# Two blocks' first layer in seven products, a written-out TensorE order, and weights released in three steps

## The chip, the cores and the metric

The kernel runs on one core of one Trainium2 chip. The metric is the device time of one execution in microseconds (us); 312.05 us is the median of five runs of the kernel before, which lie between 306.78 and 312.97 us. The profile shows one of these executions.

## What is computed

For 8 batches and 8 heads, 576 positions of 64 values each, a retention layer without softmax, then a layer with the activation h·cos(h) between two matrix products:

```python
scores = scale * np.matmul(q, k.transpose(0, 1, 3, 2))
ret = scores * Dmat[None]                 # gamma_h ** (i - j), 0 above the diagonal
x = np.matmul(ret, v)                     # then (B*S, H*D) = (4608, 512)
h = x @ w_in                              # 512 -> 2048
out = (h * np.cos(h)) @ w_out             # 2048 -> 512
```

Inputs and output are float32; the kernel multiplies in bf16 and accumulates in float32.

## The kernel before

The 4608 tokens are cut into nine blocks (0 to 8) of 512. For a block, the retention part runs as "sessions" on TensorE, chunks of 64 positions with a running state: `session` (L634 scores, L643 state update, L652 the state's share, L661 the share inside a chunk). Its operands come as float32 tiles through `stgk`, `stgv`, `stgq` (three, three and two buffers), are weighted and cast mostly on POOL (GpSimd) into `natk`, `natv`, `qnat`, and are transposed for the scores by TensorE (L575, L593) or by a DMA (L604). The result is the block's `xt`.

The first layer is `mlp1`: for each of 16 columns f of 128, four matmuls into a PSUM bank (L763, 512 or 256 columns wide; blocks 0 to 2 take it in halves of 256), then ScalarE's sine of the shifted bank (L771, which is the cosine) and VectorE's product into `gt` (L774). So the bank is read twice and free after two operations.

The second layer is `plain2` for block 0 (L800). For blocks 1 to 8 it is `wino2`: a two-by-two block product with seven block products in place of eight (P1 to P7; each 16 matmuls of 256 columns, L886). It needs sums of the left operand (four per half on VectorE, L847 and L853), sums of `w_out` made once (`wsums`, L826), and reuses three PSUM banks: ScalarE takes a copy (`sn`) of a partial sum before TensorE goes on accumulating in the bank, and VectorE adds copy and bank (L898). `store` (L785) issues the output from SP.

The order of the work is made when the kernel is built. `Graph.run` is a list scheduler: every operation has a duration and a wanted time (`prio`), an engine takes what can start first, TensorE's choice also weighs a model of its instruction fetch (`fetched`: 256 instructions at a time, taken to land 6000 ns after they are asked for, three of them 3500 ns later). The engines then run their lists in order, with semaphore waits between them. Buffers come from pools (`POOLS`); those of most pools are handed out in the order of creation. In the first 20 us `warm` (L418) fills TensorE's gaps with matmuls of ones, 128 columns each.

At the start the loads of q, k, v go through SP's queue; `w_in` (four slabs, order 0, 2, 1, 3) and `w_out` (four slabs) are issued by POOL. Slab 0 of `w_in` waits for the first half of the first v tile; the other seven all wait for the second half of the q tile of x = 1 (`graph`, L954 to L958). Here x = 0 and x = 1 are the two pairs of batches that a block takes together. The next tiles of k, q, v (rows 2 and 3) wait for slabs 1 and 3 of `w_out` (`GATE`).

## Time and profile before

| | |
|---|---|
| median of 5 runs | 312.05 us (306.78 to 312.97) |
| the profiled execution | 312.97 us; its span 311.2 us, so 1.8 us lie around the span |
| mean granted TensorE clock | 0.988 of full |
| TensorE matmuls | 295.2 us busy (95%), 4274 recorded |
| VectorE, ScalarE, POOL busy | 206.3, 188.3, 109.8 us |
| first matmul of the first layer | 20.45 us from the span's start |
| end of TensorE's last matmul | 308.0 us |

A row of the groups reads: line, engine, operation, tile written <- tiles read, shape, count | busy us, mean ns of one | idle time just before it and what ended most of it. Matmuls overlap, so a mean of 273 ns is a latency; the rate at which they follow each other is read from the chain of waits, whose rows give start, length and what ran.

### The profile page before, as it was taken

What the parts mean: (1) busy time and instruction counts of PE and PEld (TensorE: products, weight loads), DVE (VectorE), ACT (ScalarE), POOL (GpSimd) and SP (SyncE); (2) the same over time, 40 slices, a digit from 0 to 9 for tenths busy, and PEclk for the clock granted to TensorE, in tenths of its full rate; (3) what the DMA queues carried; (4) which work ended last, traced back from release to release, by engine and by line L of the source; (5) the groups of instructions that cost most, each with busy time, mean ns of one, the idle gap of its engine ahead of it and who ended that gap; (6) DMA issues with size and microseconds to landing.
All of it is one profiled execution on the core that took longest, in us unless ns stands there. A gap on an engine that the chain in (4) does not pass through costs nothing.

```text
span 311.2 us, 10091 instructions
## 1 busy us (share of the span) xinstructions
PE 295.2 (95%) x4274; PEld 215.2 (69%) x4277; DVE 206.3 (66%) x371; ACT 188.3 (61%) x340; POOL 109.8 (35%) x134
## 2 busy tenths in 40 slices
PE   8987999799999999999997799999999999999995
PEld 8876765688777888567854475768646666667684
DVE  3475972475975669898476577775679667665641
ACT  3376743888959786855463566474686765455430
POOL 2261057769627581930470731312742000000000
PEclk9999999999999999999999599999999999999999
DMA  8999999999989899875999539259802100300123
GB/s 168 213 171 206 204 227 192 245 266 222 199 207 207 122 209 263 170 156 143 249 204 264 127 32 243 67 107 200 173 1 72 69 2 0 121 16 2 61 77 136
DMA packets 126397, 46.80 MB, mean 150 GB/s; under 512 B 105104, under 2 KB 122000, under 8 KB 126352
## 3 DMA queue, kind: packets, MB, share of 16 engines
q1 hardware_dynamic: 122128, 41.95, 61.4%
q0 software_dynamic: 4224, 4.19, 8.3%
q8 instruction: 34, 0.56, 0.8%
q14 instruction: 11, 0.09, 0.1%
HBM read 36.70 MB, written 9.44 MB: 148 GB/s over the span
## 4 chain that ended last, share of the span: by engine, by line
PE 88%; ACT 3%; issue 2%; DVE 2%; DMA 2%; POOL 2%; DVEq 0%
PE bk L763 40%; PE bk L886 32%; PE bk L800 4%; PE bk L418 2%; PE bk L661 2%; PE bk L652 2%; DMA stgq<-in_q_dram 2%; PE bk L634 2%; PE st L643 2%; PE bk L575 2%; PE bk L593 1%; DVE pt L723 1%; POOL win L743 1%; POOL wout L747 1%; ACT xt L476 1%
## 5 line engine op out<-in xcount | busy, mean ns | idle before, releaser
L763 PE MATMUL bk<-xt,win 128*128 128x256 bf16 (+1 forms) x768 | 140.5, 328 | 2.3 <-issue 1.3
L774 DVE TENSOR_TENSOR gt<-bk,cb 128x256 bf16<-128x256 f32 (+1 forms) x192 | 103.6, 555 | 59.0 <-ACT cb L771 52.6
L771 ACT ACTIVATE cb<-bk,cpi 128x256 bf16<-128x256 f32 (+1 forms) x192 | 108.3, 584 | 55.8 <-PE bk L763 54.8
L763 PEld LDWEIGHTS bk<-xt,win 128*128 128x128 bf16 x768 | 72.9, 98 | 44.6 <-issue 2.7
L512 POOL TENSOR_TENSOR natv<-stgv,wv 128x512 bf16<-128x512 f32 x38 | 42.0, 1116 | 36.2 <-DMA stgv<-in_v_dram 16.6
L477 POOL CAST natk<-stgk 128x512 bf16<-128x512 f32 x36 | 22.2, 630 | 61.4 <-DMA stgk<-in_k_dram 35.3
L557 POOL TENSOR_TENSOR qnat<-stgq,wq 128x512 bf16<-128x512 f32 x36 | 38.6, 1090 | 13.9 <-DMA stgq<-in_q_dram 9.0
L723 DVE TENSOR_TENSOR pt<-bk,tri 128x512 bf16<-128x512 f32 (+1 forms) x46 | 29.6, 683 | 16.3 <-PE st L643 13.1
L476 ACT ACTIVATE sbd<-st 128x512 bf16<-128x512 f32 x32 | 19.3, 602 | 23.0 <-PE st L643 23.0
L886 PE MATMUL bk<-wout,s 128*128 128x256 bf16 x256 | 32.2, 273 | 0.0
L886 PE MATMUL bk<-tw,s 128*128 128x256 bf16 x256 | 31.6, 273 | 0.5 <-DVE s L847 0.5
L886 PE MATMUL bk<-wout,gt 128*128 128x256 bf16 x256 | 31.6, 273 | 0.0
L886 PEld LDWEIGHTS bk<-wout,s 128*128 128x128 bf16 x256 | 24.6, 98 | 6.7
L886 PEld LDWEIGHTS bk<-tw,s 128*128 128x128 bf16 x256 | 24.7, 98 | 6.1 <-DVE s L847 0.8
L886 PEld LDWEIGHTS bk<-wout,gt 128*128 128x128 bf16 x256 | 24.7, 98 | 4.6 <-DVE pt L723 0.2
L476 ACT ACTIVATE sn<-bk 128x512 f32<-128x512 f32 x24 | 14.4, 604 | 18.7 <-PE bk L886 18.7
L476 ACT ACTIVATE xt<-bk 128x512 bf16<-128x512 f32 x36 | 23.1, 695 | 0.3 <-PE bk L661 0.2
L898 DVE TENSOR_TENSOR os<-bk,sn 128x512 f32<-128x512 f32 x24 | 16.4, 684 | 7.9 <-PE bk L886 7.8
L886 PE MATMUL bk<-tw,gt 128*128 128x256 bf16 x128 | 17.3, 282 | 0.0
L418 PE MATMUL bk<-one 128*128 128x128 bf16 x181 | 14.8, 248 | 1.1 <-DVE lq L441 1.1
L886 PEld LDWEIGHTS bk<-tw,gt 128*128 128x128 bf16 x128 | 12.9, 101 | 4.2 <-issue 0.6
L643 PE MATMUL st<-natv,natk 64*64 64x64 bf16 x512 | 11.5, 195 | 4.1 <-issue 4.1
(63 smaller groups left out, 235.1 us busy)
## 6 DMA issues: line engine op xcount, KB each, us to landing
stgk<-in_k_dram SPq DMA_DIRECT2D x32, 256.0 KB, 4.9
stgv<-in_v_dram SPq DMA_DIRECT2D x32, 256.0 KB, 5.3
out_dram<-os SPq DMA_DIRECT2D x15, 512.0 KB, 3.4
stgq<-in_q_dram SPq DMA_DIRECT2D x12, 512.0 KB, 5.9
stgq<-in_q_dram SPq DMA_DIRECT2D x8, 256.0 KB, 5.6
win<-in_moe_w_in_dram POOLq DMA_DIRECT2D x4, 512.0 KB, 7.3
wout<-in_moe_w_out_dram POOLq DMA_DIRECT2D x4, 512.0 KB, 14.7
out_dram<-os SPq DMA_DIRECT2D x6, 256.0 KB, 3.5
```

Of the source, the lines that this page charges most:

```text
L418: inst = e.matmul(ap(self.at(self.wb), 512, 0, 128, 0, [1, 128]), self.ONE.ap(), self.ONE.ap(), start=True, stop=True, skip_group_check=True)
L476: return self.one(eng, dur, lambda e: e.activation(dst(), src(), AF.Copy), r=r, w=w, **kw)
L477: return self.one(eng, dur, lambda e: e.tensor_copy(dst(), src()), r=r, w=w, port=True, **kw)
L512: self.one(ve, vd, lambda e, b2=b2: e.tensor_tensor(ap(self.at(t["natv"]), 1024, 0, 128, 512 * b2, [D, H], [1, D]), ap(self.at(t["stgv"]), ...
L557: self.one("dve" if fast else "pool", 620 if fast else 990, lambda e, t=t, y=y: e.tensor_tensor(ap(self.at(t["qnat"]), 1024, 0, 128, y * 5 ...
L643: yield lambda e, b2=b2, c=c, o=o: e.matmul(ap(self.ST[u[0]], 512, 64 * ph, 64, (4 * b2 + c) * 64, [1, 64]), ap(self.at(self.keys(u)["natk ...
L723: self.one("dve", 610, lambda e, hp=hp: e.tensor_tensor(ap(self.at(pt), 1024, p0, n, 512 * hp, [64, 8], [1, 64]), ap(self.at(sc[hp]), 512, ...
L763: inst = e.matmul(ap(self.at(bk), 512, 0, 128, 0, [1, n]), ap(self.WIN, 4 * DFF, 0, 128, c * DFF + 128 * f, [1, 128]), ap(self.at(xt), 204 ...
L771: self.one("act", 70 + n, lambda e: e.activation(ap(self.at(cb), TB, 0, 128, 0, [1, n]), ap(self.at(bk), 512, 0, 128, 0, [1, n]), AF.Sin, ...
L774: self.one("dve", 75 + n / 0.96, lambda e: e.tensor_tensor(ap(self.at(gt), NF * TB, 0, 128, f * TB + 256 * h0, [1, n]), ap(self.at(bk), 51 ...
L886: inst = e.matmul(ap(self.at(bank), 512, 0, 128, 256 * tt, [1, 256]), l(f, tt), rr(f), start=(first and f == 0 and tt == 0), stop=True, sk ...
L898: self.one("dve", 610, lambda e: e.tensor_tensor(view(h, c), ap(self.at(bank), 512, 0, 128, 0, [256, 2], [1, 256]), ap(self.at(sn[name]), ...
```

## The change

- **Seven products in the first layer of blocks 7 and 8.** `mlp1w` works on four groups of four columns f. In place of 16 matmuls of 512 columns, a group has seven products of four matmuls of 256 columns each (M1, M2, M6, M5, M7, M3, M4), in three banks. ScalarE copies three partial sums into float32 buffers of `stgv` and `stgq`; VectorE adds bank and copy three times; ScalarE takes the four sines; three of the four last products run on POOL, one on VectorE. `xsums` makes four sums of `xt` per block on VectorE. `win_sums` makes the sums of `w_in` once, in eight operations on VectorE, three kinds into the three `stgk` buffers and one over `w_in` itself; the last k tiles are created before it.
- **The order on TensorE** is a written list of 412 task numbers (`ORDER`); a task's number is its place in the order of creation. The model of the fetch goes. The first 12 loads on SP keep their order. The other engines are still listed by the scheduler, with a new model of the DMA queues (`Queues`).
- **The gap filling** is worked out by `fill`, with matmuls of 512 columns.
- **Release of the weight slabs.** Slab 0 as before; slab 2 after the first half of q of x = 1; the other six after the first half of v of x = 1 (`FIRST`). The wait of rows 2 and 3 on `w_out` stays.
- **The last block's** P4 is done one token half after the other, in two banks, each copied and stored by itself.
- A write on VectorE, ScalarE or POOL now also waits for earlier readers on its own engine. `PERIOD`, `T0`, `T1` (wanted times) and `NOXBAR` have new values.

```diff
-            deps += [d for d in readers if d.eng != eng or d.sem or sem]
+            deps += [d for d in readers if d.eng != "pe" or eng != "pe"]
...
+class Queues:
+
+
+    def __init__(self):
+        self.sp, self.pool, self.held = 800.0, 0.0, []
+
+    def end(self, eng, at, dur):
+        if eng == "pool":
+            a = max(self.pool, at + 3000)
+            self.pool = a + dur
+            self.held.append((a, a + dur))
+            return self.pool
+        t = max(self.sp, at + 1100)
+        for a, b in self.held:
+            if b <= t:
+                continue
+            if t + dur <= a:
+                break
+            dur -= max(0, a - t)
+            t = b
+        self.sp = t + dur
+        return self.sp
...
+                if e == "pe" and t.idx != first or e == "sp" and lead and t is not lead[0]:
+                    continue
...
+                first = next(turn, None)
+            elif e == "sp" and lead:
+                lead.pop(0)
...
+    def fill(self):
+
+        free = {e: self.START * (e == "sp") for e in ("pe", "act", "dve", "pool", "sp")}
+        done, queues = {}, Queues()
+        for t in self.order:
+            s = free[t.eng]
+            for o, x in t.deps:
+                s = max(s, done[o][1] if o.dma is not None else done[o][0] + x + lat(o, t))
+            for b in t.bufs:
+                if b.tasks[0] is t and b.prev:
+                    s = max([s] + [done[o][1] + 90 for o in b.prev.tasks if o in done and o.eng != t.eng])
+            if t.eng == "pe":
+                at = max(free["pe"], 1150.0)
+                gap = s - at - 100
+                slow = max(0.0, min(gap, 4500 - at))
+                t.pre = max(0, int(slow / 440 + (gap - slow) / 220)) if gap > 150 else 0
+            free[t.eng] = end = s + t.dur
+            if t.dma is not None:
+                end = queues.end(t.eng, s, t.dma) + 800
+            done[t] = (s, end)
+            if t.name == "m1_0_0":
+                return
 
 
...
+    SEVEN = 7
+    TLATE = 0
+    ORDER = [int(x) for x in """3 2 0 1 9 4 5 10 6 7 8 11 14 20 16 21 12 18 13 40 32 22 23 44 39 42 19 43 45 17 33 30 37 29 15 41 26 28
+        34 31 35 24 25 92 96 38 36 93 100 97 48 27 94 98 101 46 95 102 47 103 49 104 105 99 55 50 53 106 51 107
...
+        360 366 364 365 389 386 368 367 362 387 370 392 373 390 372 369 375 391 393 371 374 377 396 380 394 379
+        397 376 378 381 382 404 395 383 400 398 399 401 402 403 405 406 407 408 409 411 410""".split()]
+    FIRST = [(0, "v", 0), (1, "q", 0), (1, "v", 0)]
+    NOXBAR = set(range(8))
+    PERIOD, T0, T1 = 27000, 19000, 29000
 
     def __init__(self, nc, es, q, k, v, w_in, w_out, out):
...
+                inst = e.matmul(self.at(self.wb).ap(), self.ONE.ap(), ap(self.ONE, 128, 0, 128, 0, [0, 4], [1, 128]),
                                 start=True, stop=True, skip_group_check=True)
...
+    def win_sums(self):
+
+        self.tv = {i: Buf("stgk") for i in (1, 2, 4)}
+
+        def b(k, n, q):
+            return ap(self.WIN, 4 * DFF, 0, 128, 2 * k * DFF + 1024 * n + 512 * q, [DFF, 2], [1, 512])
+
+        def t(i, q):
+            return self.at(self.tv[i]).ap().bitcast(BF16)[:, 1024 * q:1024 * q + 1024].rearrange("p (c f) -> p c f", c=2)
+
+        for q in range(2):
+            w0, w1 = ("win", q), ("win", 2 + q)
+            for dst, x, y, r, w in (
+                    (lambda q=q: t(1, q), lambda q=q: b(0, 1, q), lambda q=q: b(0, 0, q), [w0, w1], (self.tv[1], q)),
+                    (lambda q=q: t(2, q), lambda q=q: b(1, 1, q), lambda q=q: t(1, q), [w1, (self.tv[1], q)], (self.tv[2], q)),
+                    (lambda q=q: t(4, q), lambda q=q: b(1, 0, q), lambda q=q: t(2, q), [w0, (self.tv[2], q)], (self.tv[4], q)),
+                    (lambda q=q: b(0, 1, q), lambda q=q: b(1, 1, q), lambda q=q: b(0, 1, q), [w1], w1)):
+                self.one("dve", 610, lambda e, dst=dst, x=x, y=y: e.tensor_tensor(dst(), x(), y(), ALU.subtract),
+                         r=r, w=[w], port=True, late=self.TLATE)
...
+    def xsums(self, j):
+
+        xt, b = self.xt[j], [Buf("s"), Buf("s")]
+        self.xs[j] = b
+        keys = [(xt, h, s) for h in range(2) for s in range(2)]
+
+        def a(k, h):
+            return ap(self.at(xt), 2048, 0, 128, h * 1024 + 256 * k, [512, 2], [1, 256])
+
+        def v(i):
+            return ap(self.at(b[(i - 1) // 2]), 1024, 0, 128, 512 * ((i - 1) % 2), [256, 2], [1, 256])
+
+        for i, x, y, r, op in ((1, lambda: a(0, 1), lambda: a(1, 1), [], ALU.add),
+                               (2, lambda: v(1), lambda: a(0, 0), [(b[0],)], ALU.subtract),
+                               (3, lambda: a(0, 0), lambda: a(0, 1), [], ALU.subtract),
+                               (4, lambda: a(1, 0), lambda: v(2), [(b[0],)], ALU.subtract)):
+            self.one("dve", 400, lambda e, i=i, x=x, y=y, op=op: e.tensor_tensor(v(i), x(), y(), op),
+                     r=keys + r, w=[(b[(i - 1) // 2],)], port=True, name=f"X{i}_{j}")
+
+    def mlp1w(self, j, g, base, span):
+
+        xt, xs = self.xt[j], self.xs[j]
+        if j not in self.gt:
+            self.gt[j] = Buf("gt")
+        gt = self.gt[j]
+        A, Bb, C = Buf("bk"), Buf("bk"), Buf("bk")
+        hv, hq = Buf("stgv"), Buf("stgq")
+        at = {(0, 0): (hv, 0), (0, 1): (hv, 1), (1, 1): (hq,)}
+        sn = {"p1": at[0, 0], "u2": at[0, 1], "p5": at[1, 1]}
+
+        def view(b):
+            return ap(self.at(b[0]), 1024, 0, 128, 512 * (b[1:] == (1,)), [1, 512])
+
+        def ra(k, h):
+            return lambda c: ap(self.at(xt), 2048, 0, 128, h * 1024 + 256 * k + 128 * c, [512, 2], [1, 128])
+
+        def rs(i):
+            return lambda c: ap(self.at(xs[(i - 1) // 2]), 1024, 0, 128, 512 * ((i - 1) % 2) + 128 * c, [256, 2], [1, 128])
+
+        def lb(k, n):
+            return lambda c, f: ap(self.WIN, 4 * DFF, 0, 128, (2 * k + c) * DFF + 1024 * n + 128 * f, [1, 128])
+
+        def lt(i):
+            def at(c, f):
+                o = 1024 * (f // 4) + 512 * c + 128 * (f % 4)
+                return self.at(self.tv[i]).ap().bitcast(BF16)[:, o:o + 128]
+            return at
+
+        q = g // 2
+        w0, w1 = [("win", q)], [("win", 2 + q)]
+        kx = [(xt, h, s) for h in range(2) for s in range(2)]
+        ks = {i: [(xs[(i - 1) // 2],)] for i in range(1, 5)}
+        kt = {i: [(self.tv[i], q)] for i in (1, 2, 4)}
+        spec = {1: (lb(0, 0), ra(0, 0), w0 + kx, A, True), 2: (lb(1, 0), ra(1, 0), w0 + kx, Bb, True),
+                6: (lt(2), rs(2), kt[2] + ks[2], A, False), 5: (lt(1), rs(1), kt[1] + ks[1], C, True),
+                7: (lb(0, 1), rs(3), w1 + ks[3], A, False), 3: (lb(1, 1), rs(4), w1 + ks[4], C, False),
+                4: (lt(4), ra(1, 1), kt[4] + kx, A, False)}
+
+        def snap(name, bank):
+            self.copy("act", 490, lambda: view(sn[name]), lambda: self.at(bank).ap(), [(bank,)], [sn[name]])
+
+        def out(h, n):
+            return ap(self.at(gt), NF * TB, 0, 128, (8 * n + 2 * g) * TB + 256 * h, [TB, 2], [1, 256])
+
+        def act(h, n, bank=None):
+            cb = Buf("cb")
+            key = (bank,) if bank else at[h, n]
+            buf, o, size = key[0], int(key[1:] == (1,)), 512 if bank else 1024
+            self.one("act", 582, lambda e: e.activation(
+                self.at(cb).ap(), ap(self.at(buf), size, 0, 128, 512 * o, [1, 512]), AF.Sin, bias=self.CPI.ap(), scale=1.0),
+                r=[key, ("cpi",)], w=[(cb,)])
+            eng = "dve" if bank else "pool"
+            self.one(eng, 608 if eng == "dve" else 1120, lambda e: e.tensor_tensor(
+                out(h, n), ap(self.at(buf), size, 0, 128, 512 * o, [256, 2], [1, 256]),
+                ap(self.at(cb), TB, 0, 128, 0, [256, 2], [1, 256]), ALU.mult), r=[key, (cb,)],
+                w=[(gt, 8 * n + 2 * g + f, h) for f in range(2)], port=not bank)
+
+        def comb(h, n, bank):
+            v = at[h, n]
+            self.one("dve", 610, lambda e: e.tensor_tensor(view(v), self.at(bank).ap(), view(v), ALU.add),
+                     r=[(bank,)], w=[v])
+            act(h, n)
+
+        for n, p in enumerate((1, 2, 6, 5, 7, 3, 4)):
+            l, r, keys, bank, first = spec[p]
+
+            def mm(e, l=l, r=r, bank=bank, first=first):
+                for f in range(2):
+                    for c in range(2):
+                        inst = e.matmul(ap(self.at(bank), 512, 0, 128, 256 * f, [1, 256]), l(c, 2 * g + f), r(c),
+                                        start=(first and c == 0 and f == 0), stop=True, skip_group_check=True)
+                return inst
+
+            self.one("pe", 4 * 109, mm, ni=8, r=keys + [(hv, "begun")] * (n > 0),
+                     w=[(bank,)] + [(hv, "begun")] * (n == 0), alloc=[gt, A, Bb, C, hv, hq] if n == 0 else (),
+                     prio=base + span * n / 7,
+                     name=f"M{p}_{j}_{g}")
+            if p == 1:
+                snap("p1", A)
+            elif p == 2:
+                comb(0, 0, Bb)
+            elif p == 6:
+                snap("u2", A)
+            elif p == 5:
+                snap("p5", C)
+            elif p == 7:
+                comb(1, 1, A)
+            elif p == 3:
+                comb(0, 1, C)
+            else:
+                act(1, 0, A)
+
+    def store(self, j, half, os, cols=(0, DM), tt=None):
         c0, cn = cols[0], cols[1] - cols[0]
         g0, r0 = divmod(2 * j, NR)
         one = r0 < NR - 1
         for p0, n, gen, r in ([(0, 128, g0, r0)] if one else [(0, 64, g0, r0), (64, 64, g0 + 1, 0)]):
...
+        last = j == NTB - 1
+        A, Bb, C = [Buf("bk") for _ in range(1 + last)], [Buf("bk")], [Buf("bk")]
...
             l, rr, keys, bank, first = spec[p]
+            final = last and p == 4
             for q in range(2):
-                def mm(e, l=l, rr=rr, bank=bank, first=first, q=q):
-                    for f in range(4 * q, 4 * q + 4):
-                        for tt in range(2):
-                            inst = e.matmul(ap(self.at(bank), 512, 0, 128, 256 * tt, [1, 256]), l(f, tt), rr(f),
-                                            start=(first and f == 0 and tt == 0), stop=True, skip_group_check=True)
+                def mm(e, l=l, rr=rr, bank=bank, first=first, q=q, final=final):
+                    for f in range(8) if final else range(4 * q, 4 * q + 4):
...
+                if last:
                     self.store(j, 1, os[1], (256, 512))
-                    self.store(j, 1, os[1], (0, 256))
-                else:
+                for b, i, n in pieces(A):
+                    self.copy("act", 70 + 210 * n, lambda i=i, n=n: ap(self.at(os[1]), 1024, 0, 128, 512 * i, [512, n], [1, 256]),
+                              lambda b=b, i=i, n=n: ap(self.at(b), 512, 0, 128, 256 * i, [256, n], [1, 256]), [(b,)],
+                              [(os[1], 0, i)] if last else [(os[1], 0)])
+                    if last:
+                        self.store(j, 1, os[1], (0, 256), i)
+                if not last:
...
-        for s, x in enumerate((0, 2, 1, 3)):
-            self.load_w("win", x, gate if s >= self.LEAD else [(self.kv[0, 0, 0]["stgv"], 0)], 100 + s)
-        for s in range(4):
-            self.load_w("wout", s, gate, 200 + s)
+        for s, x in enumerate((0, 2, 1, 3, 4, 5, 6, 7)):
+            x1, n, b2 = self.FIRST[min(s, len(self.FIRST) - 1)]
+            t = self.kv[x1, 0, 0]
+            gate = [(t["stgq", b2],) if n == "q" else (t["stg" + n], b2)]
+            self.load_w("win" if s < 4 else "wout", x % 4, gate, 100 + s)
...
+            if j + 1 == self.SEVEN:
+                tiles([X(15), Y(15), X(17), Y(17)])
+                self.win_sums()
+            if not last and j + 1 >= self.SEVEN:
+                self.xsums(j + 1)
+                for g in range(4):
+                    self.mlp1w(j + 1, g, base + PER * g / 4, PER / 4)
+            elif not last:
...
```

## The prediction

> **What bounds the kernel now.** I read first the page's busy rows and slices:
>
> ```profile
> PE 295.2 (95%) x4274; PEld 215.2 (69%) x4277; DVE 206.3 (66%) x371; ACT 188.3 (61%) x340; POOL 109.8 (35%) x134
> ...
> PE   8987999799999999999997799999999999999995
> ...
> PEclk9999999999999999999999599999999999999999
> ```
>
> TensorE is busy nearly everywhere; no other engine comes near. There is one dip late, with a lowered clock beside it, and small ones in the first third. A busy matmul row is not a full one, so second the chain of waits, for the rate:
>
> ```profile
> 280.15 0.87 PE bk L886 x8
> 281.03 0.86 PE bk L763 x4
> ```
>
> A 256-column matmul takes 0.87/8 = 0.109 us of TensorE, a 512-column one 0.86/4 = 0.216. The chain is TensorE for 88% of the span. Third, the windows, for where it is not:
>
> ```profile
> 20.00:54.00 34.00, 30.97 (x316) 21.36 (x319) 21.78 (x45) 19.74 (x42) 14.01 (x16) 1.00 1.12 204
> 54.00:100.00 46.00, 42.55 (x830) 35.69 (x829) 30.43 (x63) 37.49 (x79) 30.82 (x36) 1.00 1.00 225
> 100.00:160.00 60.00, 59.90 (x990) 44.48 (x989) 45.23 (x76) 39.16 (x73) 29.57 (x33) 1.00 0.91 190
> 160.00:180.00 20.00, 15.90 (x202) 9.13 (x201) 12.93 (x18) 9.74 (x16) 10.51 (x11) 0.83 0.82 183
> 180.00:264.00 84.00, 83.91 (x1283) 55.79 (x1281) 61.12 (x91) 53.30 (x88) 19.06 (x22) 1.00 0.43 90
> 264.00:295.50 31.50, 31.50 (x227) 20.97 (x228) 20.68 (x32) 16.20 (x25) 0.00 (x0) 1.00 0.13 47
> ```
>
> (stretch, length, then busy us of TensorE, its weight loads, VectorE, ScalarE, POOL; clock; DMA share.) Until 54 us the DMA engines are full: the weights' arrival paces it. From 100 us TensorE has no idle time but in 160 to 180. The waits of TensorE name that one:
>
> ```profile
> PE st L643 <- issue: 4.1, 1, 4.1
> PE bk L634 <- POOL natv L512: 1.5, 1, 1.5
> PE bk L763 <- issue: 1.3, 1, 1.3
> ```
>
> "issue" at 168.9 us: no semaphore is late. The packet records show a 16,384-byte instruction packet on queue 8 at 170.4, 14.8 us after the one before it, and TensorE goes on at 173.0. It had issued a burst of short session matmuls and ran dry. The 1.3 at 28.5 has such a packet at 27.5.
>
> **What the Trainium skill says.** "Runtime: NRT & Kernel Launch", Instruction fetch mechanics: instructions come in blocks of 256 by a DMA queue of the sequencer's own, mostly hidden. The trace agrees with the size (34 such packets), and shows one that was not hidden. "TensorE: Matmul & The Clock Gate", What's actually happening: after an idle window of about 3.4 us the array falls to half clock and needs about as long to return. Here the 4.1 us wait is followed by 6.8 us at 0.5. "SBUF — State Buffer", SBUF: two separate sides: VectorE with two SBUF inputs and POOL exclude each other for a whole instruction. The trace agrees: the sums of L853 on `gt` alone mean 0.87 us over the kernel, 0.69 after 264 us where POOL is idle.
>
> **The change, part by part**, against the profiled execution (312.97 us, span 311.2).
>
> *Seven products.* Removed: two blocks of 64 matmuls of 0.216 us, 27.6 us. Added: 2 x 4 groups x 28 matmuls of 0.109, 24.4 us. On a saturated TensorE **−3.2 us**, which I hold firm.
>
> *What the other engines pay for it.* Durations from these rows:
>
> ```profile
> L771 ACT ACTIVATE cb<-bk,cpi 128x512 bf16<-128x512 f32 x96 | 66.0, 688 | 44.8 <-PE bk L763 44.7
> L476 ACT ACTIVATE sn<-bk 128x512 f32<-128x512 f32 x24 | 14.4, 604 | 18.7 <-PE bk L886 18.7
> L774 DVE TENSOR_TENSOR gt<-bk,cb 128x512 bf16<-128x512 f32 x96 | 65.2, 689 | 36.7 <-ACT cb L771 33.4 <-PE bk L763 2.7
> L898 DVE TENSOR_TENSOR os<-bk,sn 128x512 f32<-128x512 f32 x24 | 16.4, 684 | 7.9 <-PE bk L886 7.8
> L512 POOL TENSOR_TENSOR natv<-stgv,wv 128x512 bf16<-128x512 f32 x38 | 42.0, 1116 | 36.2 <-DMA stgv<-in_v_dram 16.6 <-PE bk L661 12.2 <-PE bk L886 7.1
> ```
>
> Per block with its neighbour's second layer, TensorE needs 12.2 + 7 x 16 x 0.109 = 24.4 us. ScalarE: 4 x (4 x 0.69 + 3 x 0.60) = 18.2, and 4 x 0.60 for `wino2`, 20.6 us (11.0 + 2.4 before). VectorE: 4 x (3 x 0.68 + 0.69) = 10.9; four sums of `xt`, half the size of L847's 0.69 and so estimated at 0.42, 1.7; `wino2` 8 x 0.69 + 3 x 0.68 = 7.6; together 20.2 us. POOL: 12 x 1.12 = 13.4 us, idle there before. All fit under 24.4, at 84, 83 and 55%. The eight sums of `w_in` (0.69 to 0.91, as L826) are 5.5 to 7.3 us of VectorE, once, around block 6, with the last sessions beside them: VectorE then has about 20.2 + 4 x 0.68 + 6.4 = 29.3 us against TensorE's 24.4 + 2 x 1.2 = 26.8, so some must fall into the period before, where it had room; six of the eight only need free `stgk` buffers, the two over `w_in` wait for block 6's last first-layer matmul. In a group, bank A passes M1, copy, M6, copy, M7, sum, M4, sine, product: 4 x 0.44 + 2 x 0.8 + 1.0 + 1.7 = 6.1 us, a group's own period; the written order lays P products between (374, then 377, 396, 380, 394, 379, 397, then 376: 3.9 us from M7 to M4), and a second group can use other banks of six. The end: after M3 of the last group (382) stand 7 pieces, 6.5 us, before P6's second half, against sum, sine, POOL product and two sums, 0.7 + 0.7 + 1.1 + 1.4 and 0.7 of hand-offs = 4.6. Covered. What this adds in waits no trace of before shows: none at best, 10 us if every group waits 1.2 us. I take **+2**.
>
> *The fetch.* The stall is 4.1 us, and half clock for 6.8 us costs up to 3.4 more: 7.5. The fastest of the five runs is 6.2 below the profiled one, so such stalls come and go. Whether a written order keeps bursts away from block ends can't be seen in the profile; the count of instructions is about the same (+2 x 96 for the products, −2 x 130 or so for wider gap filling). Between 0 and −7.5; I take **−4.5**, as the order keeps long products around sessions.
>
> *Order between 48 and 100 us.* TensorE ran 19 matmuls of `plain2` from 49.8 to 54.2 while two of the transposes for rows 2 of x = 0 stood behind them, though POOL had made the last of their operands by 49.7. Then it idled: start-to-start times against the rates above leave 3.9 us lost in 50 to 60, 2.0 in 60 to 70, 3.3 in 80 to 100. The list has the transposes 46 to 49 between pieces 94 to 103 of `plain2`, and nine first-layer pieces of x = 0 (66 to 60) ahead of the first session of x = 1 (57). Between 0 and −7: **−3.5**.
>
> *Slab releases.* Slab 2 is asked for when the first half of q of x = 1 lands (16.4, its first reader) rather than behind slab 0's followers at 18.9; slabs 1, 3 and `w_out` wait for v, which was first read at 22.0 under their own traffic and should come at about 20. POOL issues six of them in 6 x 0.8 us ahead of its own `natv`, as before. The DMA work up to 54 us is the same, and rows 2 and 3 still wait for it. −2 to +2; I take **−0.5**, for the 1.5 us wait on `natv` at 22.3.
>
> *The end.* Copy 0.60 becomes 0.38 (256 columns), the last store halves: **−0.4** of the 3.2 us after the last matmul. The waits on an engine's own readers, the smaller changes of `w_in`'s order and `NOXBAR` (rows 7 lie in tiles that rows 6 had already put on TensorE) cost nothing I can find: in-order engines have passed those readers; uncovered, some 0.1 us each.
>
> Sum: −3.2 + 2 − 4.5 − 3.5 − 0.5 − 0.4 = −10.1, so 302.9 against the profiled execution. That is the slowest of the five and probably has more stall than the median; against the median of 312.05 I allow 9.6: **302.5 us**.
>
> **Rivals.** (B) *The fetch stays late* (28%): the stall only moves to another burst. For it: the DMA queues are as full as before until 230 us, and a written list cannot move when a packet lands. Then half the gain of the order from 48 to 100 goes the same way: −3.2 + 2 − 1.8 − 0.5 − 0.4 = −3.9, 308 us. (C) *The group's hand-offs bound the last two blocks* (9%), slower: POOL's products and VectorE's two-input sums shut each other out, `stgv` and the three banks come free late, and the next group's M1, in a fixed order, stops all P products behind it. At 9 us a group in place of 6.1, 8 x 2.9 = 23 us on the forecast without its 2 us: 324. Its side of the 2% begins at 8.3 us a group. Against it: 83% loads and the distances above. (D) *Nearly all waits go* (9%): −3.2 − 7.5 − 6 − 0.5 = −17.2, 295 us. The forecast has 54%.
>
> 2% is about what a measurement of this kernel can tell from no change: below 305.8 is faster, above 318.3 slower. Faster: D and most of the forecast, 0.59. Same: B and the rest of it, 0.33. Slower: most of C, 0.08. The range from 296 to 311 leaves out C and most of D; the forecast's own is 298 to 307.
>
> **What would show it.** Right: L763 with 128 fewer 512-column matmuls and 224 of 256 columns at 0.109 in the chain; no "issue" wait of TensorE over 1.5 us and the clock at 0.99 or more throughout; TensorE 98% busy in 54 to 100; first-layer groups of blocks 7 and 8 within 6.5 us. Wrong: an "issue" wait at another session (B); TensorE waiting for ScalarE copies, POOL products or sums of `w_in` in the last 65 us (C); a later start of the first layer, which would turn the slab release into a loss.

## The result and the profile after

The changed kernel takes 311.27 us in the median of 43 runs (307.36 to 316.68); the kernel before, in the runs beside it, 309.88 in the median of 80 (306.25 to 315.44). The ratio is 1.0077, 95% interval 1.0059 to 1.0095: no gain, rather a small loss. That comparison leaves out the runs over 1.5% above their kernel's fastest, 38 of the kernel before (all but one of its upper group) and 16 of the changed one; with all runs in, the means are 311.57 and 310.23, a ratio of 1.004. The times of the kernel before form two groups, 37 of 80 below 309 us and 39 above 310. The profiled execution of the changed kernel took 310.32 us, its span is 308.5.

The page's busy rows and slices of the changed kernel, to be laid beside those of before:

```profile
PE 292.4 (95%) x4234; PEld 213.7 (69%) x4238; DVE 216.6 (70%) x388; ACT 199.3 (65%) x367; POOL 138.9 (45%) x158
...
PE   8968999979999999899999999999999999999996
...
PEclk9999999999999999999999999999999999999999
```

The late dip and its lowered clock are gone. There are new nicks instead in slices 9 and 17. The chain of waits has both kinds of first-layer matmul, with the rates that the prediction used:

```profile
163.60 1.73 PE bk L804 x8
273.20 2.18 PE bk L929 x20
```

1.73/8 = 0.216 us for 512 columns, 2.18/20 = 0.109 for 256. The windows, with the columns of the table of before (stretch, length, busy us of TensorE, its weight loads, VectorE, ScalarE, POOL; clock; DMA share; GB/s):

```profile
54.00:100.00 46.00, 42.59 (x805) 35.26 (x807) 29.63 (x62) 35.38 (x74) 30.05 (x36) 1.00 0.97 220
100.00:160.00 60.00, 57.75 (x978) 42.99 (x976) 42.34 (x74) 38.92 (x72) 27.67 (x32) 1.00 0.90 182
160.00:180.00 20.00, 19.28 (x283) 11.54 (x284) 14.69 (x22) 12.04 (x19) 11.72 (x12) 1.00 1.04 200
180.00:264.00 84.00, 82.41 (x1291) 58.10 (x1287) 66.64 (x103) 55.12 (x93) 27.04 (x28) 1.00 0.44 90
264.00:295.50 31.50, 31.45 (x286) 27.09 (x283) 26.03 (x36) 24.50 (x42) 20.51 (x18) 1.00 0.14 52
```

From 160 to 180 us TensorE is busy 3.4 us more than before. Nothing is won in 54 to 100 (42.55 before), and two stretches that were full before are no longer: 100 to 160 lost 2.15 us, 180 to 264 lost 1.5. In the last stretch TensorE has no idle time, though VectorE, ScalarE and POOL now work there. The waits of TensorE:

```profile
PE bk L804 <- ACT xt L517: 2.3, 4, 0.8
PE bk L616 <- issue: 1.6, 1, 1.6
PE bk L675 <- issue: 1.4, 1, 1.4
PE bk L804 <- DMA win<-in_moe_w_in_dram: 1.3, 1, 1.3
```

Two waits named "issue" (67.6 and 124.5 us) stand in stages that had none, and first-layer pieces (L804) wait four times for the copy of a session's result. What the new work costs on the other engines:

```profile
L912 POOL TENSOR_TENSOR gt<-stgv,cb 128x512 bf16<-128x512 f32 x16 | 20.5, 1284 | 28.3 <-ACT cb L908 26.5
L908 ACT ACTIVATE cb<-stgv,cpi 128x512 bf16<-128x512 f32 x16 | 11.5, 721 | 5.6 <-DVE stgv L919 5.5
L919 DVE TENSOR_TENSOR stgv<-bk,stgv 128x512 f32<-128x512 f32 x16 | 10.9, 684 | 4.5 <-PE bk L929 4.5
L517 ACT ACTIVATE stgv<-bk 128x512 f32<-128x512 f32 x16 | 9.5, 591 | 2.0 <-PE bk L929 1.7
```

They are what the prediction took (1.12, 0.69, 0.68, 0.60) but for POOL's product, which is a seventh longer.

**Two tools for what follows.** A *ledger*: the time passed, less the TensorE work done so far, gives the time that TensorE has lost. The work is counted at 0.216 us for a matmul of 512 columns, 0.109 for 256, 0.056 for a transpose of 128 and 0.0095 for one of 64 columns; gap filling counts as lost. And the *places* of the "issue" waits. Counting two instructions for each matmul (weights and product) and one for each separate semaphore wait, every "issue" wait of TensorE over 0.3 us after 60 us, in every run, is within about ten instructions of a position n x 256 + 195 of its stream: block 20 for the 168.9 us wait of before, blocks 6 and 14 for the two of after, and 11 for a third of 0.35 us at 104.0; 3.7 us together. The packet of 16,384 bytes on queue 8 lands some 1.4 us before TensorE goes on. So these look like late instruction packets, at fixed ends of blocks of 256. *Half clock* below means a granted TensorE clock of 0.5.

### The profile page after: what moved, and what is told of

Its sections match the earlier page's. It is cut to its first block, busy times and chain, and to the rows that moved or that the text cites. A ratio compares the mean times of both kernels' runs of the same rounds, so it can differ in the third digit from the quotient of the medians.

```text
span 308.5 us, 10055 instructions
## 1 busy us (share of the span) xinstructions
PE 292.4 (95%) x4234; PEld 213.7 (69%) x4238; DVE 216.6 (70%) x388; ACT 199.3 (65%) x367; POOL 138.9 (45%) x158
## 4 chain that ended last, share of the span: by engine, by line
PE 79%; DVE 6%; DMA 5%; ACT 4%; issue 3%; SPq 2%; POOL 0%; DVEq 0%; ACTq 0%
PE bk L1062 30%; PE bk L804 28%; PE bk L929 8%; DMA stgv<-in_v_dram 5%; PE bk L974 4%; DVE gt L815 3%; PE bk L675 2%; ACT xt L517 2%; PE bk L693 2%; PE st L684 2%; PE bk L616 2%; PE bk L702 1%; ACT sbd L517 1%; PE bk L634 1%; SPq L591 1%
## 5 line engine op out<-in xcount | busy, mean ns | idle before, releaser
L815 DVE TENSOR_TENSOR gt<-bk,cb 128x256 bf16<-128x256 f32 (+1 forms) x160 | 81.8, 529 | 51.1 <-ACT cb L812 39.7
L804 PE MATMUL bk<-xt,win 128*128 128x256 bf16 (+1 forms) x640 | 105.7, 315 | 4.4 <-ACT xt L517 2.3
L812 ACT ACTIVATE cb<-bk,cpi 128x256 bf16<-128x256 f32 (+1 forms) x160 | 85.1, 563 | 32.4 <-PE bk L804 31.2
L804 PEld LDWEIGHTS bk<-xt,win 128*128 128x128 bf16 x640 | 60.0, 98 | 37.5 <-ACT xt L517 2.5
L518 POOL CAST natk<-stgk 128x512 bf16<-128x512 f32 x36 | 21.6, 624 | 65.8 <-PE st L684 33.7
L912 POOL TENSOR_TENSOR gt<-stgv,cb 128x512 bf16<-128x512 f32 x16 | 20.5, 1284 | 28.3 <-ACT cb L908 26.5
L1062 PE MATMUL bk<-wout,s 128*128 128x256 bf16 x256 | 32.8, 273 | 0.0
L517 ACT ACTIVATE sbd<-st 128x512 bf16<-128x512 f32 x32 | 19.2, 601 | 20.1 <-PE st L684 19.9
L517 ACT ACTIVATE sn<-bk 128x512 f32<-128x512 f32 (+1 forms) x26 | 14.6, 570 | 12.6 <-PE bk L1062 12.6
L1081 DVE TENSOR_TENSOR os<-bk,sn 128x512 f32<-128x512 f32 (+1 forms) x25 | 16.6, 665 | 5.3 <-PE bk L1062 5.2
L1062 PE MATMUL bk<-tw,gt 128*128 128x256 bf16 x128 | 16.4, 273 | 0.0
L517 ACT ACTIVATE kt<-bk 128x512 bf16<-128x512 bf16 x20 | 11.8, 601 | 7.0 <-PE bk L616 5.7
L908 ACT ACTIVATE cb<-stgv,cpi 128x512 bf16<-128x512 f32 x16 | 11.5, 721 | 5.6 <-DVE stgv L919 5.5
```

What stands on the lines that cost most here:

```text
L517: return self.one(eng, dur, lambda e: e.activation(dst(), src(), AF.Copy), r=r, w=w, **kw)
L518: return self.one(eng, dur, lambda e: e.tensor_copy(dst(), src()), r=r, w=w, port=True, **kw)
L804: inst = e.matmul(ap(self.at(bk), 512, 0, 128, 0, [1, n]), ap(self.WIN, 4 * DFF, 0, 128, c * DFF + 128 * f, [1, 128]), ap(self.at(xt), 204 ...
L812: self.one("act", 70 + n, lambda e: e.activation(ap(self.at(cb), TB, 0, 128, 0, [1, n]), ap(self.at(bk), 512, 0, 128, 0, [1, n]), AF.Sin, ...
L815: self.one("dve", 75 + n / 0.96, lambda e: e.tensor_tensor(ap(self.at(gt), NF * TB, 0, 128, f * TB + 256 * h0, [1, n]), ap(self.at(bk), 51 ...
L912: self.one(eng, 608 if eng == "dve" else 1120, lambda e: e.tensor_tensor(out(h, n), ap(self.at(buf), size, 0, 128, 512 * o, [256, 2], [1, ...
```

## The experiments

The theory at the start: the seven products pay, and late instruction packets and waits of the new order take their gain away. The rival: the products themselves cost it, by what they ask of VectorE, ScalarE and POOL. A ratio is to the kernel before, run beside it on the same chip. "Old listing" means the old `Graph` with its model of queues and fetch, its filling, wanted times and slab release, and no waits on an engine's own readers.

### First set: before again, and the parts of the change

**The kernel before again**, for a second trace.

> The kernel before, unchanged, for a second profile. The first one held a 4.1 us wait on TensorE's own instructions at 168.9 us and 6.8 us of half clock after it. If that wait comes and goes from one execution to the next, a span near 305.5 us with a clock of 1.0 is about what an execution without it shows, and the rest of the profile is the same to within 1 us. If it belongs to the order of the kernel, it stands at the same place again.

308.86 us, span 307.1, 1.6 more than expected; two stretches of half clock, at 26 and 60 us, stand in it. There is no "issue" wait at block 20. TensorE's longest wait is another, early one:

```profile
PE bk L634 <- POOL natv L512: 1.8, 1, 1.8
```

The packet of block 20 landed 5.5 us after TensorE had come to within 25 instructions of the end of the block before it, while in the first trace it took 10.4 us. This stall comes and goes in one and the same program.

**New order, plain first layer**: the seven products taken out of the changed kernel.

```diff
-            if not last and j + 1 >= self.SEVEN:
+            if False:
```

(`win_sums` goes as well, and `ORDER` has four plain pieces in a group's places)

> The changed kernel with the first layer of blocks 7 and 8 done plainly again (16 columns f of four 512-column matmuls; no sums of w_in and xt), each group's four f in the places of its 1st, 3rd, 5th and 7th product in the written order; all else as changed. Theory A, the seven products save their 3.2 us and the loss lies in the order: about 1.2 to 1.3% slower than before plus 0.8, so a ratio near 1.018. Theory B, the seven products lose to waits in the last 70 us what they save on TensorE: ratio 1.006 to 1.010, as the changed kernel. Theory C, they are the loss itself: ratio 1.00 or less.

Median 313.37, ratio 1.020 (1.013 to 1.027); the changed kernel stands 1.2% below. That is what the first theory expects: the seven products pay, and the rest of the change costs. With all runs in, though, the means of this run and of the kernel before beside it are 313.64 and 311.39, a ratio of 1.007, which is too near the changed kernel's 1.004 to show it. The light loads below decide.

**Old order, plain, in the new listing.** The same, and `ORDER` holds the order that the old scheduler makes.

> The changed kernel with the first layer of blocks 7 and 8 done plainly again and TensorE's list as the kernel before had it, task for task; the slab releases, gap filling, queue model, waits on the engine's own readers and the split end stay as changed. Theory A, the written order is what loses: a ratio of 1.000 or below (0.4 us of the end gained). Theory D, the releases and the other small parts lose it: ratio 1.010 to 1.018. If the instruction waits belong to the order, this one has again the occasional wait near 169 us.

313.91, ratio 1.020 (1.013 to 1.026), no better than the new order, so the written order alone doesn't explain the loss. Its trace has 3.3 us of "issue" at 124 us with half clock behind it, 0.95 at 104.5 and 0.87 at 90.

**Old order to the first piece of block 7, then the new one.**

> The changed kernel with the seven products, TensorE's list up to the first task of block 7's first layer as the kernel before had it, and after that the written order's. If the written order loses in its first 230 us (some 4 us between 100 and 130) and the seven products gain: 0.985 to 0.993. If the loss is in the last 70 us: 1.000 to 1.005.

315.53, ratio 1.026 (1.019 to 1.032): "issue" waits of 1.55 us at 87 and 3.3 at 127, with half clock around the first and after the second. Both forecasts missed. Three different orders have three different sets of late packets.

### Second set: where the block ends fall

**Old order, plain, narrow filling**, so that the sessions lie on the instruction positions of before; and **the changed kernel with 42 and with 168 more instructions** in the filling, which moves all block ends by as many.

```diff
+            if self.NARROW > 0:
+                self.NARROW -= 1
+                narrow += 4
```

(four fillers of 128 columns for one of 512, `NARROW` 7 and 28 times)

> As the run with the old list and the plain first layer, but the 42 gap fillers of 512 columns are each four of 128 columns, and the first group has 13 more: 4277 matmuls on TensorE, as the kernel before, so every session again lies against the blocks of 256 instructions as it did there (8725 instructions on TensorE; before 8726; without the edit 8447). Theory F, the loss is instruction fetch, set by where the block ends fall in the list: the waits at 104 and 124 us vanish and the ratio falls from 1.0195 to 0.995 to 1.003. Theory D, releases, queue model or waits on own readers: 1.015 to 1.02 as before.

> The changed kernel with seven of its gap fillers of 512 columns cut into four of 128: the same filling time, 42 TensorE instructions more, so that every block of 256 ends 42 instructions earlier in the work. In the changed kernel's trace the time that a block takes, with the waits taken out, falls under 5.2 us at 5 block ends before 235 us; moved by 42 it does at two. Theory F: the waits at 67, 104 and 124 us shrink or vanish, 2 to 3 us faster than the changed kernel (ratio to before 0.998 to 1.002). If the fetch is not what costs: 1.008 as it was.

> The changed kernel with 28 fillers cut into four: 168 TensorE instructions more at no filling time, block ends 168 earlier. Now ten blocks before 235 us would take 1.2 to 4.5 us. Theory F: many waits on instructions, each at a block end, and 8 to 20 us slower than the changed kernel (ratio 1.03 to 1.07). If the fetch is not what costs: 1.008 as it was.

Ratios 1.013 (1.008 to 1.019), 1.012 (1.002 to 1.023), 1.014 (1.004 to 1.024). All three forecasts from the places of the block ends missed (0.995 to 1.003, 0.998 to 1.002, 1.03 to 1.07); the last was far off, as I had taken every landing as late. With 42 more, the wait at block 6 grows to 4.65 us; with 168 more it goes, and one of 4.1 us stands at block 13. Moving the ends moves the waits and does not remove them, and a packet's lateness differs from place to place.

**The old slab release** in the changed kernel.

```diff
-    FIRST = [(0, "v", 0), (1, "q", 0), (1, "v", 0)]
+    FIRST = [(0, "v", 0), (1, "q", 1)]
```

> The changed kernel with the release of the weight slabs as before (slab 0 with v of x = 0, all others with the second half of q of x = 1); TensorE's list and its number of instructions unchanged. If the three releases are worth what the prediction took, 0.5 us slower than the changed kernel (1.0095); if they are the loss, 1.000. Between 1.004 and 1.012 they don't matter.

Median 310.21 of 20, ratio 1.009 (1.006 to 1.011), the changed kernel's within the interval. The three releases show no effect; from the two intervals, the old release costs 0.3 us, give or take 1, so the predicted 0.5 is not excluded either.

### Third set: the old listing around old and new order

My theory was now that the new listing of the loads and other engines made the packets late.

> Nothing of the change is left but the last block's tail and the earlier creation of the last four tiles: TensorE's old order, plain first layer, and also the old listing of the other engines (old model of the DMA queues, old filling, old wanted times, old slab release, no waits on an engine's own readers). Theory 1 (the listing of the loads and of the other engines moves the instruction packets, and this is why the old order in the new listing lost 1.3 to 2.0%): ratio 0.997 to 1.003, and TensorE's loss outside half clock at 300 us below 41 us. Theory 2 (the listing is innocent; the tail or the tiles, or chance in the packets, cost it): ratio 1.010 to 1.020 again.

> The run with the old listing, and the seven products alone added to it in the old order, a group's products spread over the places of its four old pieces. Both theories give the products 3.2 to 3.7 us here as they did in the new listing: theory 1 then expects a ratio of 0.986 to 0.992 to the kernel before, the best of all so far; theory 2 expects 1.000 to 1.010. If the groups need the new order's spacing in blocks 7 and 8, waits on copies, sums and POOL products in the last 65 us eat 2 us or more of it: 0.995 and up in theory 1.

> The old listing with the written TensorE order, plain first layer: the order alone. Theory 1, with the waits inside stages that the order's ledger showed (4 to 5 us lost after 60 us, 2 us gained before): ratio 1.005 to 1.015. If the order is worth what the prediction gave it (3.5 us) and only the new listing spoils it: 0.985 to 0.992. Theory 2: 1.015 to 1.025.

> The changed kernel with the old listing of the loads and of the other engines: written order and seven products kept. Theory 1: 3.7 us below the run before it in this list, ratio 0.993 to 1.003, so 0.5 to 1.5% better than the changed kernel's 1.008. Theory 2: 1.005 to 1.012, as the changed kernel.

| order, first layer (old listing) | median | ratio (95%) |
|---|---|---|
| old, plain | 313.28 | 1.020 (1.015 to 1.025) |
| old, seven products spread | 317.13 | 1.032 (1.026 to 1.037) |
| new, plain | 318.04 | 1.033 (1.028 to 1.038) |
| new, seven products | 314.24 | 1.022 (1.017 to 1.027) |

None came out as theory 1 expected, so it falls; only the first came out as theory 2 had it. It follows the kernel before (second trace) in the ledger up to 120 us (34.0 lost against 33.2). Then it waits 1.7 us for a VectorE sum at 126 us, and its packet of block 20 is late (2.1 us, then half clock). The second run (its profiled execution is the longest of six) tells of rival C, the group's hand-offs:

```profile
PE bk L902 <- DVE stgq L892: 2.3, 3, 1.3
PE bk L902 <- ACT stgv L490: 1.6, 5, 0.5
```

Between 240 and 300 us it loses 8.6 us, the plain one 1.5: with a group's seven products simply put in the places of its four old pieces, TensorE does wait for copies and sums, and loses some 7 us more. In the written order the same window shows a single wait, of 0.2 us. And the written order needs the new listing: with the old one it has lost 37.4 us by 100 us, with the new one 31.3 (plain layer in both). Which part of the listing does it was not tried.

### Fourth set: empty queues

To take the lateness of packets away without touching any list, the loads of rows from 4 on bring one head of eight (q from row 8 on). The other heads keep old data, so the values are not the reference's; the work of the engines is the same:

```diff
+            nh = H if gen == 0 and R < 2 else 1
...
-                    bass.AP(self.src[src], at, [[D, n], [S * D, H], [1, D]])),
+                    bass.AP(self.src[src], at, [[D, n], [S * D, nh], [1, D]])),
```

> The kernel before, but the loads of k, v and q from row 4 on (q from row 8 on) bring one head of eight; the other heads keep old data, so the values are not the reference's. TensorE's list and all other lists are the same. Load theory (an instruction packet is late because the DMA queues are full of loads): every packet after 60 us lands within 4 us, no instruction wait, no half clock; all runs sit with the fast ones of the kernel before, ratio 0.985 to 1.000. Place theory (a packet is late because a burst of short matmuls ends its block early, whatever the queues carry): the wait at 168.9 us stays in about half of the runs and the times keep their two groups, 307 and 312.5 us.

> The changed kernel with the same cut of the loads. Load theory: the 3.7 us of instruction waits at the three block ends go, 311.3 becomes 306 to 308.5 us, ratio 0.995 to 1.002; beside the kernel before with light loads it is then within 1% of it. Place theory: 3 us or more of instruction waits remain and the ratio stays over 1.003.

> The written order with the plain first layer and light loads. It stands 3.2 to 3.9 us above the changed kernel with light loads if the seven products are worth the same without instruction waits. Beside the kernel before with light loads it gives the order and the new listing without the waits for instructions: load theory expects +1 to +4 us, the waits inside the stages that the ledger shows; if the order itself costs nothing and only instructions were late, 0 to +0.5 us.

Medians of 22 runs each: before 307.08 (306.38 to 309.17), changed 307.05 (306.45 to 309.16), new order with plain layer 309.95 (309.09 to 314.73); ratios 1.000 (0.998 to 1.002), 1.000 (0.998 to 1.002), 1.007 (1.005 to 1.010). The windows of before and changed kernel with light loads:

```profile
54.00:100.00 46.00, 42.69 (x830) 35.67 (x829) 29.88 (x63) 37.24 (x79) 30.41 (x36) 1.00 0.33 93
100.00:160.00 60.00, 59.90 (x991) 44.62 (x989) 44.53 (x76) 39.07 (x73) 30.81 (x35) 1.00 0.44 95
160.00:180.00 20.00, 20.00 (x370) 12.98 (x368) 16.48 (x27) 13.86 (x23) 9.43 (x10) 1.00 0.42 77
180.00:264.00 84.00, 83.94 (x1173) 55.56 (x1172) 60.10 (x89) 52.30 (x85) 17.74 (x20) 1.00 0.21 55
```

```profile
54.00:100.00 46.00, 43.88 (x815) 35.97 (x814) 30.51 (x63) 36.82 (x78) 30.55 (x36) 1.00 0.33 90
100.00:160.00 60.00, 59.08 (x986) 43.62 (x984) 43.60 (x76) 39.40 (x73) 30.01 (x34) 1.00 0.47 94
160.00:180.00 20.00, 19.51 (x365) 12.50 (x362) 15.95 (x24) 12.77 (x22) 8.76 (x10) 1.00 0.42 83
180.00:264.00 84.00, 82.41 (x1206) 58.13 (x1204) 66.27 (x102) 55.86 (x95) 28.35 (x28) 1.00 0.22 54
```

The DMA share of 54 to 100 falls from 1.0 to 0.33. No "issue" wait is left after 60 us in either kernel, and the upper group of the kernel before is gone. So the loads in the queues make the packets late. The load theory holds, and both ratios are in the expected ranges, though packets took up to 5.8 us where I had written 4. How late decides how long TensorE stands, at one and the same block end (landing counted as above):

| block end near 68 us, new order | packet lands after | TensorE waits |
|---|---|---|
| light loads | 4.2 us | 0 |
| changed kernel | 5.4 us | 1.77 us |
| three pieces moved (below) | 6.3 us | 2.39 us |
| old middle (below) | 6.6 us | 2.67 us |

| block end near 170 us, old order | packet lands after | TensorE waits |
|---|---|---|
| before, light loads | 5.0 us | 0 |
| before, second trace | 5.5 us | 0 |
| old listing, plain | 8.3 us | 2.1 us |
| old listing, seven spread | 8.7 us | 2.6 us |
| before, first trace | 10.4 us | 4.1 us |

Without late packets the rest of the change is bare: the seven products are worth 309.95 − 307.05 = 2.9 us (3.2 to 3.9 expected), and the new order, with its listing, the moved tiles and the new end, costs 309.95 − 307.08 = 2.9 us. So the products are not what costs, and the rival of the start falls.

### Fifth set: where the order loses

The ledger of TensorE's lost time, us:

| lost by | 60 | 100 | 130 | 170 | 240 | 300 us |
|---|---|---|---|---|---|---|
| before, light loads | 25.5 | 31.3 | 32.9 | 33.7 | 35.3 | 36.8 |
| new order, plain, light | 23.1 | 29.7 | 32.1 | 33.1 | 37.8 | 40.2 |
| changed, light | 23.8 | 30.4 | 32.8 | 33.7 | 38.2 | 41.3 |
| old middle, light (below) | 23.6 | 30.1 | 32.5 | 33.2 | 36.0 | 38.8 |

By 60 us the written order is 2.4 us ahead, by 170 only 0.6, and from there to 240 it loses 4.7 us against 1.6. First I moved three second-layer pieces up behind a session, ahead of the first-layer piece that waited there for `xt` or a bank (0.70, 0.85 and 0.73 us at 105, 216 and 235 us):

```diff
-... 123 168 145 152 133 ...        273 298 280 285 ...        304 274 303 301 ...
+... 123 168 169 145 152 ...        273 298 299 280 ...        304 303 274 301 ...
```

> The changed kernel with three second-layer pieces (the second halves of P4 of block 1, P7 of block 5 and P4 of block 5) moved up to stand directly behind a session, so that the next block's first piece does not wait for the copy of xt or for a bank. If these waits (0.70, 0.85 and 0.73 us in the trace of the changed kernel) are what the written order costs there, they go and the time falls by 1.5 to 2.3 us: ratio about 1.001 to 1.004. If something else is late behind them (sums, banks), the time stays within 0.5 us: 1.006 to 1.010.

311.70, ratio 1.011 (1.004 to 1.018): missed. The three waits are gone, but new ones stand up to 18 us behind them (1.4 us at 124, 0.3 at 228, 0.8 at 239). TensorE's longest waits of this kernel in 100 to 245 us are

```profile
PE bk L1062 <- DVE s L1021: 1.4, 1, 1.4
PE bk L1062 <- DVE gt L815: 0.8, 1, 0.8
PE bk L675 <- DVE gt L815: 0.4, 1, 0.4
```

The third, at 180 us, was in the changed kernel too. VectorE's sums and products are now the late ones. Then I put the whole stretch from 143 to 239 us back to the old order, the written order before and after it:

> The changed kernel, but between 143 and 239 us TensorE takes its pieces in the order of the kernel before; the written order stands before and after this stretch. If the order's loss lies there (with light loads 170 to 240 us lost 4.7 us in the written order against 1.6 in the old one), 2 to 3 us come back: 308 to 309.5 us, ratio 1.000 to 1.004 to the kernel before, if the instruction waits stay as they are (their block ends at 68, 104 and 124 us lie ahead of the edit). If the old stretch costs the same once the rest is changed, or brings its own late packet at 169 us: 311 us and more.

> The same with light loads (from row 4 on one head of eight is loaded, values not the reference's), so without late packets. Order theory: 2 to 3 us below the changed kernel with light loads (307.05), so 304 to 305 us, below the kernel before with light loads (307.08) by nearly the seven products' 2.9 us; ratio 0.990 to 0.994. Otherwise 306.5 to 307.5 us.

With light loads 305.11 us (304.86 to 305.89), ratio 0.991 (0.986 to 0.997), in the expected range of ratios: 1.9 us under the changed kernel with light loads and 2.0 under the kernel before with them. These ran on another chip, but the ranges of times don't touch. With the old middle, TensorE is busy 83.46 us of the stretch of 180 to 264 us:

```profile
180.00:264.00 84.00, 83.46 (x1221) 60.09 (x1220) 68.85 (x103) 56.53 (x95) 30.62 (x30) 1.00 0.20 56
```

With full loads it takes 309.08 (307.74 to 310.86), 2.2 us under the changed kernel's median, ratio 1.004 (0.998 to 1.011), as expected. The interval overlaps the changed kernel's (1.006 to 1.010) and takes in 1, so with full loads it is shown to beat neither kernel: TensorE waited 2.7 us for the packet at 68 us, with half clock after it (0.96 in the window of 54 to 100).

## Why the prediction was wrong

The predicted 302.5 us missed by 8.8, and the range ended just under the median. The change itself was off by 11.0 (−9.6 predicted, +1.4 measured); 2.2 of this are hidden because the kernel before fell from 312.05 in five runs to 309.88 in eighty, which was luck. Term by term:

| term | predicted | measured | by |
|---|---|---|---|
| seven products, with the waits they add | −3.2 + 2 | −2.9 | light loads, with and without them |
| late fetch | −4.5 | +1.4 | 311.27 − 307.05 = 4.2 after; 309.88 − 307.08 = 2.8 before |
| order | −3.5 | +2.9 | light loads, new order plain against before (with its listing) |
| slab releases | −0.5 | −0.3, give or take 1 | the run with the old release |
| end | −0.4 | −0.4 | 2.8 us from the last matmul to the end of the span, 3.2 before |

Products, fetch and order give +1.4, the difference of the medians 311.27 − 309.88. That they do is no test: the three differences are built to add up so, and whatever else light loads change is counted as fetch. (The end and the releases are inside the row of the order.)

*The seven products* were right in mechanism and sign. −3.2 of work is there; the mis-sized part is the 2 us of waits: the ledger has 1.1 by 300 us (41.3 against 40.2). −3.2 + 1.1 fits the two profiled executions, 307.65 − 309.81 = −2.2; the medians give 0.7 more. A group does take longer than the 6.5 us that I gave as a sign, 6.2 to 11.3 us from its first to its last matmul, but other pieces fill it. Rival C did not come about, because of the order; the run with the old order shows that its mechanism is real, at some 7 us.

*The fetch* is one of two steps that failed, by 5.9 us. I priced it from one execution that had the whole stall, against 312.97 us, and wrote that "the order keeps long products around sessions". The stall at 168.9 us did go, and with it 3.4 us in the window of 160 to 180. But 7.5 us was too much even for one execution: the 6.8 us of half clock began at 171.0, two us before TensorE went on, and so cost at most 2.4 us. From 130 to 240 us the first trace of before loses 8.7 us in the ledger and the second 3.0, so the stall cost 5.7. And by the two groups of times it exists in about half of the runs, which leaves some 2.8 us to win on the mean, as the light loads have it. The new order then brought its own late packets, at 68, 104 and 124 us, 3.7 us in the profiled run. Rival B, "the stall only moves to another burst", was the right one, and its 308 us still too good. What I could have read from the trace of before is that its DMA share was 1.0 from 54 to 100 and 0.91 to 160, so that a burst of session matmuls could be caught there too.

*The order* is the other step, off by 6.4 us. My 3.5 us were taken from the idle time of 48 to 100 us, and up to 60 us the written order does bring 2.4. I then treated the rest of the list as unchanged. It changes every stage, and from 170 to 240 us, where before TensorE lost 1.6 us, it loses 4.7. The runs with the old middle show that this belongs to the stretch's order: 1.9 of the 2.9 us come back without late packets (2.2 with them, which is not clear of the noise). The other 1.0 is not divided among the rest of the order, the listing and the moved tiles. Which single hand-off starts it I can't say; moving three pieces only handed the waits on. Nor do I know why the old order in the old listing, which differs from before in the tail, the place of the last four tiles and a session time of 33.6 in place of 31 in the scheduler, waits 1.7 us on a sum at 126 us.

Of the signs I named, no "issue" wait over 1.5 us, TensorE 98% busy in 54 to 100 (92.6%) and groups within 6.5 us were not met; the clock (1.0 in the profiled execution), the last stretch without waits and the start of the first layer (20.1 us, not later than 20.45) were.

## What to carry to other kernels

Before a stall is counted as a gain, ask in how many executions it is there: one profile of a kernel whose times form two groups shows one group. A stretch of half clock that begins within a wait costs only what lies behind the wait. When a new order is written out for one stage, price it in every stage that it touches, above all where TensorE had no idle time. And where bursts of short matmuls run under full DMA queues, instructions are a load like any other: fewer bytes in those queues took the late packets from both kernels, while moving the block ends, in the two places tried, only moved the wait.

## What the runs showed of the hardware

- TensorE ran out of instructions (waits over 0.3 us, after 60 us) only at fixed places of its stream, a multiple of 256 instructions plus about 195. The Trainium skill, "Runtime: NRT & Kernel Launch", Instruction fetch mechanics, has blocks of 256 and calls the cost of a boundary mostly hidden; here that depends on the landing against the work left in the block: near 68 us a landing of 4.2 us was hidden and 5.4 to 6.6 cost 1.8 to 2.7 us; near 170 us 5.5 was hidden and 8.3 to 10.4 cost 2.1 to 4.1.
- The landing follows the load of the DMA queues. With a share of 0.31 to 0.47 from 54 to 180 us (light loads), packets took at most 5.8 us, counted as above; with about 0.8 to 1.05 (full loads), up to 10.4.
- Half clock came in stretches of 3.4 or 6.8 us, and no single wait as long as the 3.4 us of the prediction was needed: it came at or behind "issue" waits of 2.1 us (old listing, plain), 2.7 (old middle) and 4.1 us (before), and not behind one of 2.39 us (three pieces moved). So the length of the wait alone does not decide it.
- POOL's product of two SBUF operands and VectorE's sum of two (L1021 and L1027, 128x1024) held each other up. In the changed kernel from 240 to 300 us, a sum took 0.67 to 0.69 us where no such product was running when it began (12 sums) and 0.92 to 1.65 where one was (8). A product took 1.15 to 1.17 us alone and up to 1.61 where a sum was running. In the last stretch, 264 to 295.5 us, neither was on TensorE's path, which has no idle time there.
